# Loads of the float64 weight pieces begun by the POOL engine on a queue of its own instead of the sync engine's queue

## The chip, the cores and the metric

One core of a Trainium2 chip runs the kernel: TensorE (PE) multiplies, VectorE (DVE) and ScalarE (ACT) do elementwise work, GpSimd (POOL) does small extra work, and SyncE (SP) does nothing but start transfers. All of them work on one on-chip memory; 16 DMA engines move data between it and the chip's main memory. The metric is the device time of one execution in microseconds, lower is better.

## The reference, cut to what matters

```python
def _attn_ref(q, k, v, n_sink, window):          # 4 x 8 heads, 768 positions, 64 wide
    scores = scale * np.matmul(q, k.transpose(0, 1, 3, 2))
    keep = is_sink | in_window                   # 4 sinks, window of 128
    scores = np.where(keep, scores, -1000000000.0)
    ... # softmax
    return np.matmul(a, v).astype(np.float32)

x = attention output as 3072 tokens x 512
h = np.maximum(x @ w_in, 0.0)                    # 512 -> 2048
x = (h * h @ w_out).astype(np.float32)           # 2048 -> 512
a = x @ w1; b = x @ w2                           # 512 -> 1024 each
h = a * b @ w3                                   # 1024 -> 1024
out = (h @ w_out2).astype(np.float32)            # 1024 -> 512
```

q, k and v arrive as float32. All weights arrive as float64.

## The kernel before, in words

The kernel runs attention, the first feed-forward network and the second one for all 3072 tokens, in blocks of up to 512 tokens. The work overlaps: attention of later tokens runs on PE, DVE and ACT while the first network already works on block 0 (from about 100 to 200 us), and while blocks 1 and later follow (to about 687 us). Between about 687 and 760 us weights of the second network are folded together, and from there to the end the second network runs.

[...] `f32_piece` (L1015 to L1030) takes a buffer named `raw64` and starts the transfer of one piece of 512 x 128 float64 numbers (512 KB, read as pairs of int32) into it. `conv` then makes float32 numbers of it with `f64_to_f32_up` (L80 to L99): ACT takes the upper word (L86), DVE makes exponent and sign from the 16-bit parts (L91 and L94), and DVE joins them (L97). `split` then makes two float16 parts of the result, a high and a low one, and these are what PE multiplies with. Every second `w_in` piece has its low part made by POOL (L801).

There are two `raw64` buffers, so the transfer of a piece can start only when the piece two before it has been read by ACT (L86) and DVE (L94). 64 pieces go this way: 16 of `w_in`, 16 of the first `w_out`, 8 of the second `w_out`, and 24 of `w1`, `w2` and `w3` together. The even pieces of `w3` have a loader of their own (`load_w3`, L1176, buffer `raw_w`), which the change doesn't touch.

All transfers of the kernel are started by SP, in one order: the loads of q, k and v (L506, L518), the transposing transfers of keys (L555), of queries (L594) and of the softmax weights (L738), the weight pieces (L1029), a spill and a reload, and the output. An instruction of SP that waits holds up all that stand behind it. The same is true of POOL, which clears parts of `vp` (L599), copies the sink columns of the keys (L612, L615, L947) and makes the low parts (L801).

Line 288 is a helper: PE, ACT and DVE instructions that go through it are listed under that line, whatever they do, so they are told apart by the names of their tiles. Of these, `hps` is the first network's hidden product, `sc` the attention scores, `pr` and `stt` the softmax with its statistics, `ph` its result in float16, `pt` the transpose of `ph`, `y` the attention output and `xn` its normalized form (made by DVE, which frees the bank in which the next `y` is summed up). The helper also keeps PE, ACT and DVE in the order of the program from block 0 of the first network on. The conversions call the engines directly, and their place among the rest is chosen by a scheduler that plays the program through with a model of each engine's times; so is the order on SP and POOL.

Of the kernel before, what the change touches and what calls it, by code (L numbers as in the profile page):

```python
# [296 lines left out]
def kernel(  # L297
# [16 lines left out]
    POOL, SP = nc.gpsimd, nc.sync  # L314
# [51 lines left out]
    with ExitStack() as fast:  # L366
# [6 lines left out]
        def slab(tag, shape, dt, name, bufs=1):  # L373
            return big.tile(shape, dt, tag=tag, name=name, bufs=bufs)
# [642 lines left out]
        def f32_piece(src, dst=None, name="cv"):  # L1017

            if src.dtype == F32:
                if dst is None:  # L1020
                    dst = slab("t2", [128, 512], F32, name, bufs=T2B)
                SP.dma_start(out=dst, in_=src)
                return dst
            raw = slab("raw64", [128, 512, 2], I32, "raw64", bufs=2)
            fl = raw.rearrange("p n c -> p (n c)")
            sb32 = src.bitcast(I32)
            if len(sb32.shape) == 3:
                fl = fl.rearrange("p (a c) -> p a c", a=sb32.shape[1])
            SP.dma_start(out=fl, in_=sb32)  # L1029
            return raw  # L1030

        def conv(raw, dst=None):
# [15 lines left out]
        def load_wi(j):  # L1048
            raw_w["wi", j] = f32_piece(
                w_in[:, j * 128:(j + 1) * 128].rearrange("(c p) f -> p c f", p=128)  # L1050
            )
# [9 lines left out]
        def load_wo(j):  # L1061
            raw_w["wo", j] = f32_piece(w_out[j * 128:(j + 1) * 128, :])
# [87 lines left out]
        def load_wo2(j):  # L1150
            raw_w["wo2", j] = f32_piece(w_out2[j * 128:(j + 1) * 128, :])
# [269 lines left out]
        for h in range(2):  # L1421
            SP.dma_start(
                out=vsf[h * NSINK:(h + 1) * NSINK, :, h, :],
                in_=v[0].rearrange("(a h2) s d -> h2 s a d", h2=2)[h, 0:NSINK],
# [193 lines left out]
```

## Time and profile before

| | us |
|---|---|
| median of 3 runs (lowest to highest) | 1110.32 (1108.42 to 1110.94) |
| the profiled execution | 1110.19 |
| its span in the trace | 1108.0 |
| PE busy | 1045.3 (94%) |
| DVE busy | 750.3 (68%) |
| ACT busy | 709.4 (64%) |
| POOL busy | 45.0 (4%), 163 instructions |

The profile is of one execution. Its span runs from the first to the last instruction, and 2.2 us of the execution lie outside it. Busy time of an engine is the time in which it worked on instructions; the start of a transfer isn't counted in it. Where the trace shows idle time ahead of an instruction, it names what ended last before it could begin: "[2.26 <-DMA raw]" reads "idle for 2.26 us, until the transfer into `raw` had landed". The trace drops the numbers at the end of buffer names and the 64 of `raw64`, so `raw<-in_moe_w_out_dram` is a weight piece.

### The profile page before, as it was taken

How to read it: one execution, taken by the hardware profiler on the slowest of the kernel's cores; microseconds unless marked ns; L12 is line 12 of the kernel's file. 1: busy time of each engine (PE TensorE's matmuls, PEld its weight loads, DVE VectorE, ACT ScalarE, POOL GpSimd, SP SyncE). 2: the span in 40 equal slices, each digit the busy share in tenths (PEclk: the TensorE clock that was granted, in tenths of full speed). 3: DMA queues.
4: the chain of work that ended last, by engine and by line, in shares of the span. 5: the costliest groups of instructions: out<-in, count | busy, mean ns of one | idle time of the engine just before them, and what ended most of it. 6: DMA issues, size and time to landing. Idle time of an engine off the chain costs nothing. (4 is left out here: it accounts for less than half of the span.)

```text
span 1108.0 us, 20449 instructions
## 1 busy us (share of the span) xinstructions
PE 1045.3 (94%) x7146; PEld 636.4 (57%) x7146; DVE 750.3 (68%) x2292; ACT 709.4 (64%) x1836; POOL 45.0 (4%) x163
## 2 busy tenths in 40 slices
PE   6777897999999999999999998999999999999996
PEld 5665443555555555555554444457767776777774
DVE  8797888887788888877865667945363636453433
ACT  6975688887667666766754877854464546454532
POOL 2110111000000000000000000000000000000000
PEclk9867999999999999999999999999999999999998
DMA  8876787786567657556833324421020201010101
GB/s 189 157 157 140 179 204 184 150 183 122 104 144 145 117 107 173 118 114 144 147 68 99 115 96 140 164 75 40 2 77 1 77 1 39 1 39 1 38 1 41
DMA packets 265535, 113.46 MB, mean 102 GB/s; under 512 B 237648, under 2 KB 254032, under 8 KB 264784
## 3 DMA queue, kind: packets, MB, share of 16 engines
q1 hardware_dynamic: 265136, 111.55, 43.7%
q8 instruction: 58, 0.95, 0.4%
q14 instruction: 53, 0.43, 0.2%
q10 hardware_dynamic: 288, 0.52, 0.1%
HBM read 62.08 MB, written 11.53 MB: 66 GB/s over the span
## 5 line engine op out<-in xcount | busy, mean ns | idle before, releaser
L288 PE MATMUL hps<-xT,wi 128*128 128x512 f16 x1152 | 270.9, 386 | 0.0
L288 PE MATMUL x1ps<-g,wo 128*128 128x512 f16 x1152 | 265.6, 380 | 3.0 <-ACT g L288 2.0
L288 PE MATMUL cps<-x1T,w 128*128 128x256 f16 x2016 | 231.5, 273 | 7.2 <-DVE cq L288 4.6
L288 PEld LDWEIGHTS <-w 128*128 128x128 f16 x2016 | 196.9, 98 | 44.5 <-issue 9.1
L288 PEld LDWEIGHTS <-wi 128*128 128x128 f16 x1152 | 115.0, 100 | 123.2 <-issue 8.6
L288 PEld LDWEIGHTS <-wo 128*128 128x128 f16 x1152 | 109.8, 98 | 122.6 <-issue 5.7
L288 PE MATMUL ops<-w,h 128*128 128x512 f16 x576 | 133.5, 379 | 1.8 <-ACT h L288 1.8
L288 ACT ACTIVATE cp<-cps 128x256 f32<-128x256 f32 x96 | 36.1, 376 | 131.3 <-PE cps L288 131.3
L288 ACT ACTIVATE r<-hps 128x512 f32<-128x512 f32 x96 | 56.8, 592 | 94.7 <-PE hps L288 94.7
L288 ACT ACTIVATE pr<-pr,stt 128x264 f32<-128x264 f32 (+1 forms) x176 | 77.6, 483 | 32.9 <-DVE stt L288 31.5
L288 PEld LDWEIGHTS <-h 128*128 128x128 f16 x576 | 56.2, 98 | 58.1 <-ACT h L288 2.1
L288 DVE TENSOR_TENSOR ph<-pr,ph 128x512 f16<-128x512 f32 (+2 forms) x148 | 59.2, 436 | 35.2 <-ACT ph L288 33.2
L288 DVE SCALAR_TENSOR_TENSOR asb<-cq,cps 128x256 f32<-128x256 f32 x48 | 20.2, 420 | 87.6 <-PE cps L288 87.6
L288 DVE CUSTOM_DVE_ANT_0 pr<-sc,mask 128x264 f32<-128x264 f32 (+1 forms) x176 | 65.2, 400 | 16.1 <-PE sc L288 15.5
L288 PEld LDWEIGHTS <-pt 128*128 128x128 f16 x956 | 40.3, 98 | 34.5 <-issue 17.1
L288 ACT ACTIVATE ph<-pr 128x512 f16<-128x512 f32 (+2 forms) x148 | 55.9, 421 | 5.8 <-DMA pt<-ph 3.4
L288 ACT ACTIVATE g<-r 128x512 f16<-128x512 f32 x88 | 55.3, 629 | 2.4
L288 DVE TENSOR_TENSOR g<-r,g 128x512 f16<-128x512 f32 x56 | 38.6, 689 | 24.6 <-ACT g L288 24.4
L97 DVE SCALAR_TENSOR_TENSOR cvy<-cvy,cvt 128x512 int32<-128x512 int32 x72 | 49.1, 688 | 8.5 <-ACT cvy L86 8.3
L288 PE MATMUL y<-vp,pt 128*128 128x65 f16 (+1 forms) x888 | 40.6, 195 | 14.7 <-DVE xn L288 14.6
L288 DVE TENSOR_TENSOR h<-asb,h 128x512 f16<-128x512 f32 x48 | 33.2, 691 | 28.2 <-ACT h L288 28.2
L288 PEld LDWEIGHTS <-qT 128*128 128x128 f16 x592 | 41.4, 99 | 18.9 <-issue 0.7
(193 smaller groups left out, 1490.3 us busy)
## 6 DMA issues: line engine op xcount, KB each, us to landing
raw<-in_moe_w_out_dram SPq DMA_DIRECT2D x24, 512.0 KB
raw<-in_moe_w_dram SPq DMA_DIRECT2D x24, 512.0 KB
raw<-in_moe_w_in_dram SPq DMA_DIRECT2D x16, 512.0 KB
raw<-in_k_dram SPq DMA_DIRECT2D x84, 64.0 KB
raw<-in_q_dram SPq DMA_DIRECT2D x84, 64.0 KB
raw<-in_v_dram SPq DMA_DIRECT2D x84, 64.0 KB
x_dr<-x1e SPq DMA_DIRECT2D x20, 256.0 KB
x1s<-x_dr SPq DMA_DIRECT2D x5, 1024.0 KB
```

Of the source, the lines that this page charges most:

```text
L97: nc.vector.scalar_tensor_tensor(out=dst, in0=y, scalar=3, in1=t, op0=ALU.logical_shift_left, op1=ALU.bitwise_or)
L288: r = f(*args, **kw)
```

## The change

One line of `f32_piece` changes. The loads of the 64 pieces are started by POOL and no longer by SP. What is read, the buffers, the conversions and all other transfers stay as they are.

```diff
             sb32 = src.bitcast(I32)
             if len(sb32.shape) == 3:
                 fl = fl.rearrange("p (a c) -> p a c", a=sb32.shape[1])
-            SP.dma_start(out=fl, in_=sb32)
+            POOL.dma_start(out=fl, in_=sb32)
             return raw
```

On POOL, the instructions of the first half of block 0 (about 112 to 136 us) are these before: `vp` is cleared, and `ks` and `kT` are the sink columns of the keys.

```order
L615 COPY kT_1601<-ks_705 128x4x8
L599 MEMSET vp_1810 128x2x2
L599 MEMSET vp_2429 128x2x2
L615 COPY kT_2011<-ks_914 128x4x8
L612 COPY ks_1908<-kT_1804 128x32
L615 COPY kT_1806<-ks_1908 128x4x8
```

After the change the same stretch of POOL reads as follows.

```order
L615 COPY kT_1601<-ks_705 128x4x8
L1029 DMA raw64_1620<-in_moe_w_out_dram 128x1024
L599 MEMSET vp_1810 128x2x2
L1029 DMA raw64_1721<-in_moe_w_out_dram 128x1024
L1029 DMA raw64_1731<-in_moe_w_in_dram 128x4x256
L599 MEMSET vp_2429 128x2x2
L1029 DMA raw64_1824<-in_moe_w_out_dram 128x1024
L615 COPY kT_2011<-ks_914 128x4x8
L612 COPY ks_1908<-kT_1804 128x32
L615 COPY kT_1806<-ks_1908 128x4x8
L1029 DMA raw64_1927<-in_moe_w_out_dram 128x1024
L1029 DMA raw64_1937<-in_moe_w_in_dram 128x4x256
```

Six loads have come in between the six small instructions, in the order of the pieces; the small instructions keep their order.

On SP, the stretch of block 0 from about 146 to 160 us reads as follows before. `kT`, `qT` and `pt` are transposing transfers, `raw_2102` are pieces of q, k and v, and `raw64` the weight pieces.

```order
L555 DMA_TRANSPOSE kT_2011<-pkk_1911 128x4x128
L555 DMA_TRANSPOSE kT_2013<-pkk_1911 128x4x128
L594 DMA_TRANSPOSE qT_2015<-pkq_1912 128x4x128
L738 DMA_TRANSPOSE pt_1960<-ph0_101 128x4x128
L1029 DMA raw64_2032<-in_moe_w_out_dram 128x1024
L1029 DMA raw64_2133<-in_moe_w_out_dram 128x1024
L506 DMA raw_2102<-in_k_dram 128x2x64 x2
L506 DMA raw_2102<-in_q_dram 128x2x64 x2
L506 DMA raw_2102<-in_v_dram 128x2x64 x2
L1029 DMA raw64_2143<-in_moe_w_in_dram 128x4x256
L738 DMA_TRANSPOSE pt_2061<-ph1_102 128x9x128
```

After the change the same stretch, with its first instructions and some more at its end:

```order
L555 DMA_TRANSPOSE kT_2013<-pkk_1911 128x4x128
L594 DMA_TRANSPOSE qT_2015<-pkq_1912 128x4x128
L738 DMA_TRANSPOSE pt_1960<-ph0_101 128x4x128
L506 DMA raw_2102<-in_k_dram 128x2x64 x2
L506 DMA raw_2102<-in_q_dram 128x2x64 x2
L506 DMA raw_2102<-in_v_dram 128x2x64 x2
L738 DMA_TRANSPOSE pt_2061<-ph1_102 128x9x128
L555 DMA_TRANSPOSE kT_2216<-pkk_2118 128x4x128
L555 DMA_TRANSPOSE kT_2218<-pkk_2118 128x4x128
L594 DMA_TRANSPOSE qT_2220<-pkq_2119 128x4x128
```

The weight pieces are gone from SP, and the other transfers stand as they did. `raw64_2032` no longer stands behind the transposes.

On DVE, the start of the program (about 10.5 to 13.5 us) has the masks and the first softmax, and the first piece's conversion behind them, before:

```order
L288 TENSOR_SCALAR mask_143<-m0_135 128x128
L288 TENSOR_SCALAR mask_147<-m2_133 128x264
L288 SCALAR_TENSOR_TENSOR vp_532<-raw_171,vp_532 128x2x64
L288 TENSOR_SCALAR mask_145<-m1_134 128x264
L288 ISA pr_229,stt_230<-sc_225,mask_143 128x128
L288 ISA stt_230 128x1
L288 ISA pr_229,stt_230<-sc_227,mask_143 128x128
L288 ISA stt_230 128x1
L288 TENSOR_SCALAR stt_230<-stt_230 128x2
L91 TENSOR_SCALAR cvt_238<-raw64_183 128x512
L94 TENSOR_SCALAR cvt_238<-raw64_183 128x512
```

After the change the conversion of the first piece stands a few rows further up, and that of the second piece stands among the masks:

```order
L288 TENSOR_TENSOR m0_135<-m2_133,snk_130 128x128
L288 TENSOR_SCALAR vs_1089<-sel_78 128x4
L91 TENSOR_SCALAR cvt_249<-raw64_185 128x512
L94 TENSOR_SCALAR cvt_249<-raw64_185 128x512
L288 COPY m2_133<-snk_130 128x8
L288 TENSOR_TENSOR m1_134<-m2_133,snk_130 128x128
L288 MEMSET m1_134 128x8
L288 TENSOR_SCALAR mask_143<-m0_135 128x128
L97 SCALAR_TENSOR_TENSOR cvy_248<-cvy_248,cvt_249 128x512
L288 TENSOR_SCALAR mask_147<-m2_133 128x264
L288 TENSOR_SCALAR mask_145<-m1_134 128x264
L288 ISA pr_229,stt_230<-sc_225,mask_143 128x128
```

Two conversions (`raw64_183` and `raw64_185`) have moved ahead of the first softmax, the row `pr_229`.

## Rows read from the trace of the kernel before

**Rows 1.** Busy time by stretch: us, PE, PEld, DVE, ACT, POOL, PEclk, DMA share, GB/s.
```profile
100.00:200.00 100.00, 85.67 (x572) 43.62 (x570) 86.88 (x279) 79.32 (x234) 10.29 (x24) 0.95 0.80 183
200.00:560.00 360.00, 360.00 (x2625) 192.33 (x2624) 291.06 (x1004) 256.84 (x656) 19.39 (x88) 1.00 0.67 135
560.00:687.00 127.00, 124.20 (x653) 58.01 (x649) 79.07 (x198) 87.90 (x193) 0.00 (x0) 1.00 0.33 95
687.00:760.00 73.00, 68.03 (x384) 38.94 (x385) 56.13 (x107) 47.17 (x100) 0.00 (x0) 0.98 0.37 130
```
**Rows 2.** Waits, 100 to 200 us: who waited for whom, us in total, times, longest.
```profile
PE y L288 <- DVE xn L288: 13.4, 5, 3.6
DVE cvt L91 <- DMA raw<-in_moe_w_out_dram: 9.8, 5, 2.9
```
**Rows 3.** Timeline of DVE, conversions: start, us, instruction, idle before it.
```profile
115.34 0.46 DVE L94 TENSOR_SCALAR cvt<-raw 128x512 uint16<-128x512 uint16 x1
123.19 0.47 DVE L91 TENSOR_SCALAR cvt<-raw 128x512 uint16<-128x512 uint16 x1 [2.26 <-DMA raw<-in_moe_w_out_dram]
...
146.50 0.44 DVE L94 TENSOR_SCALAR cvt<-raw 128x512 uint16<-128x512 uint16 x1
156.22 0.47 DVE L91 TENSOR_SCALAR cvt<-raw 128x512 uint16<-128x512 uint16 x1 [2.48 <-DMA raw<-in_moe_w_out_dram]
...
175.63 0.45 DVE L94 TENSOR_SCALAR cvt<-raw 128x512 uint16<-128x512 uint16 x1
184.59 0.47 DVE L91 TENSOR_SCALAR cvt<-raw 128x512 uint16<-128x512 uint16 x1 [2.94 <-DMA raw<-in_moe_w_out_dram]
```
**Rows 4.** Timeline of SP's queue, starts of transfers in block 0.
```profile
115.14 2.50 SPq L555 DMA_TRANSPOSE kT<-pkk  x2
117.74 1.21 SPq L594 DMA_TRANSPOSE qT<-pkq  x1
119.05 0.52 SPq L1029 DMA_DIRECT2D raw<-in_moe_w_out_dram  x1
...
152.21 1.05 SPq L1029 DMA_DIRECT2D raw<-in_moe_w_out_dram  x2
...
180.44 0.52 SPq L1029 DMA_DIRECT2D raw<-in_moe_w_out_dram  x1
```
**Rows 5.** Timeline of PE, the first two of the five waits for xn.
```profile
109.52 0.81 PE L288 MATMUL y<-vp,pt 128*128 128x65 f16 x12 [3.60 <-DVE xn L288]
...
132.17 0.34 PE L288 MATMUL y<-vp,pt 128*128 128x65 f16 x6 [2.79 <-DVE xn L288]
```
**Rows 6.** Timeline of POOL in block 0.
```profile
110.63 2.41 POOL L801 TENSOR_TENSOR wi<-cvy,wi 128x512 f16<-128x512 f32 x1 [10.46 <-ACT wi L288]
...
117.45 0.12 POOL L599 MEMSET vp<- 128x4 f16 x1 [4.26 <-PE y L288]
```
**Rows 7.** Groups by line and form: count, busy, mean ns of one, idle before.
```profile
L801 POOL TENSOR_TENSOR wi<-cvy,wi 128x512 f16<-128x512 f32 x8 | 10.7, 1337 | 46.1 <-ACT wi L288 46.1
...
L97 DVE SCALAR_TENSOR_TENSOR cvy<-cvy,cvt 128x512 int32<-128x512 int32 x72 | 49.1, 688 | 8.5 <-ACT cvy L86 8.3
```
**Rows 8.** Timeline of the start, SP's queue and DVE.
```profile
8.65 0.94 SPq L1029 DMA_DIRECT2D raw<-in_moe_w_in_dram  x2
...
12.30 0.28 DVE L288 CUSTOM_DVE_ANT_0 pr<-sc,mask 128x128 f32<-128x128 f32 x1
```
**Rows 9.** Waits of DVE, 0 to 100 us, the largest line.
```profile
DVE cvt L91 <- DMA raw<-in_moe_w_in_dram: 4.7, 3, 2.1
```
**Rows 10.** Timeline of DVE in block 0, two multiplications of one shape.
```profile
111.32 1.76 DVE L288 TENSOR_TENSOR ph<-pr,ph 128x512 f16<-128x512 f32 x2
...
158.10 0.78 DVE L288 TENSOR_TENSOR ph<-pr,ph 128x512 f16<-128x512 f32 x2
```
**Rows 11.** Timeline of the fold, SP's queue and ACT.
```profile
687.15 3.64 SPq L1029 DMA_DIRECT2D raw<-in_moe_w_dram  x2
...
695.69 0.68 ACT L86 ACTIVATE cvy<-raw 128x512 f32<-128x512 f32 x1
```

## The prediction

> **What bounds the kernel now.** I read the table of stretches first. From 200 to 560 us PE is busy for all 360.00 us, so nothing that happens to a weight piece there can shorten the time [rows 1]. The stretch that is open is 100 to 200 us, block 0 of the first network beside the rest of attention: PE is busy for 85.67 of 100 us, DVE for 86.88, ACT for 79.32, POOL for 10.29. No engine is full, so it is bound by waits between engines, with DVE nearest to full. The list of waits then says whom PE waits for there: for `xn` of DVE, 13.4 us in five waits [rows 2], nearly all of the 14.33 us in which PE is not busy. In the same list DVE waits 9.8 us, five times, for a weight piece to land. DVE works in order, so an `xn` behind a waiting conversion is late.
>
> Why are these pieces late? The timelines of DVE and SP side by side tell. The second-last conversion ahead of a wait frees the buffer, at the end of its L94: 115.34 + 0.46 = 115.80, 146.50 + 0.44 = 146.94, 175.63 + 0.45 = 176.08 [rows 3]. SP begins the loads that need these buffers at 119.05, 152.21 and 180.44 [rows 4], so 3.25, 5.27 and 4.36 us later. Until then it stands in order behind other transfers: ahead of 119.05 behind two transposes of keys (2.50 us) and one of queries (1.21 us). From its begin to DVE's use a load takes 123.19 - 119.05 = 4.14, 4.01 and 4.15 us [rows 3, 4].
>
> **The change part by part.** *Removed from SP.* SP no longer begins the weight pieces. Its remaining transfers stand in the old order, each up to about 0.5 us earlier per load removed [rows 4]; I count nothing for it, since PE waits for no transpose in the list of waits' large lines.
>
> *Added to POOL.* A load is now begun by POOL, which is free for 90 of 100 us of block 0 [rows 1]. In its order each load stands behind small instructions only, so POOL is mostly there when the buffer comes free. What a begin by POOL costs more than one by SP, call it e, no row shows. The lower end is 0 (it starts as SP's, 0.52 us [rows 4]); the upper end is POOL's longest instruction in block 0, 2.41 us [rows 6]; I take the mean of its wide instruction, 1.34 us [rows 7], since preparing a transfer over 128 partitions is nearest to a piece of work over 128 partitions.
>
> Gain of each wait: the smaller of the wait and (the delay less e).
> - 123.19: wait 2.26, delay 3.25 less 1.34 = 1.91. Gain 1.91.
> - 156.22: wait 2.48, delay 5.27 less 1.34 = 3.93. Gain 2.48.
> - 184.59: wait 2.94, delay 4.36 less 1.34 = 3.02. Gain 2.94.
> - The other two waits are 9.82 - 7.68 = 2.14 us together (five waits, of which three have rows) [rows 2, 3]. I take half, 1.07.
>
> That is 8.40 us on DVE. Not all of it is seen by PE: its first waits for `xn` are at 109.52 and 132.17 [rows 5], and none lies in the 8.98 us behind 123.19, so PE had work then, and the 1.91 us are not counted. What is left is 6.5 us (6.49). With e = 0 the same sum is 2.48 + 2.94 + 2.14 = 7.6; with e = 2.41 it is 2.48 + 1.95 = 4.4, the small ones gone. What is late next is DVE itself, 86.88 us of work in what would be some 93 us.
>
> *The start.* Two conversions move ahead of the first softmax on DVE: four passes of about 0.46 us and two of 0.69 us [rows 3, 7], 3.2 us. The first softmax, at 12.30 before [rows 8], is later by up to that. The work is then missing further on; as no row of the first 100 us stands here but DVE's waits, I take DVE's share of idle time from the stretch next to it (13 of 100 [rows 1]) and a little more for the gaps of a start: a fifth of 3.2 us is not given back, +0.6. The ends: +3.2 if none is given back, and -4.7 if the three waits for `w_in` pieces in the first 100 us all go [rows 9] because the pieces start earlier than SP's 8.65 [rows 8].
>
> *POOL and DVE at once.* The same form of DVE multiplication takes 1.76 us for two at 111.32 and 0.78 us at 158.10 [rows 10]; at 111.32 POOL's L801 is running, from 110.63 for 2.41 us instead of its mean 1.34 [rows 6, 7]. So a wide POOL instruction and a DVE multiplication lengthen each other, by 1.0 us. Does a load's begin do that too? 18 pieces are begun in block 0. At the lower end none meets, 0; at the upper end all do, 18.0 us. I take a third of them, 6, at the 0.12 us of POOL's small memset [rows 6], as what a begin writes is nearer to that than to a 128x512 tile: +0.7.
>
> A rule of the Trainium skill speaks against the change here. "SBUF — State Buffer", section "SBUF: two separate sides", says in its box on the DVE-blocks-DMA trap that a transfer begun by GpSimd has its descriptors written by GpSimd, which cannot write them while DVE runs certain two-port operations, and advises a begin from ACT or SP. The pair of rows on `ph` agrees that the two engines hold each other up, and no run here shows it for a begin. By that rule the upper end of this term is the right one.
>
> *POOL's own work behind waiting loads.* POOL now waits in its queue for buffers. Behind such a wait stand memsets of `vp` and copies of sink columns. The memset at 117.45 waited 4.26 us for PE itself [rows 6], so it keeps its time as long as the load ahead of it begins at 115.80. Zero; a few tenths if not.
>
> *Later stretches.* 200 to 560 us: zero, PE is full [rows 1]. 560 to 687 us: PE is busy 124.20 of 127 us, which leaves 3 us to lose or gain. Fold: the second of the two loads at 687.15 to 690.79 is used at 695.69 [rows 11], at least 4.9 us after its begin and so 0.8 us more than the 4.1 a load takes; 1.34 is 0.5 us over that. PE idles 5 of 73 us there [rows 1], and the pieces are not what it waits for, so +0.2, with ends 0 and +1.
>
> *Sum.* Against the profiled execution, 1110.19 us (span 1108.0, and 2.2 outside), which is 0.1 us below the median of the runs: 1110.2 - 6.5 + 0.6 + 0.7 + 0.2 = **1105.2 us**. Its own range by these ends is 1098 (-7.6 and -4.7) to 1109 (-4.4 and +3.2).
>
> **The rivals.** *The transfer lands later, by as much as it begins earlier.* If a load of POOL takes 4.1 us longer to land, twice what SP's takes, the gains are 5.27 - 4.1 = 1.2 and 4.36 - 4.1 = 0.3, and pieces that just arrive now begin to be waited for, at about the same price: 1110 us, within 1108 and 1112. For it: the two queues share 16 DMA engines that are busy 80% of block 0 [rows 1], and no row shows a load by POOL. Against it: the engines are no busier than before, and what SP lost was time in line.
>
> The Trainium skill, "DMA: Bandwidth & Descriptors", section "Issuing engines are not separate DMA queues", says that starting transfers on several engines saves only the sequencer's time to start them, usually small beside the transfer. Taken as SP's own begin of 0.52 us per bound load it would give 2.6 us at most, so about 1108, which is this rival. The trace speaks half against it: it is SP's place in line, 3.25 to 5.27 us, that is long.
>
> *DVE and POOL hold each other up (the slower side).* If every begin costs a DVE instruction what L801 cost at 111.32, 1.0 us, DVE has 86.9 + 18.0 = 104.9 us of work in block 0's 100, so the stretch grows by 5 us and the gain is gone; the loads of the first 100 us add some 2 us. 1117 us. It decides from (100 - 86.9) / 18 = 0.7 us per load on. For it: the pair of rows; DVE is busy nearly always, so each begin meets something. Against it: L801 reads and writes whole tiles, a begin doesn't.
>
> *The load isn't begun earlier.* POOL could be held in its order by its own waits (for PE, for a transposed `kT`) as SP is by its transposes, or the two conversions moved ahead cost 3.2 us for good: 1109 to 1114. The order speaks against the first, as the loads stand behind copies that ran long before.
>
> **How the numbers follow.** Forecast 0.45, later landing 0.22, held up 0.25, not begun earlier or something else 0.08. A measurement of this kernel tells about 0.2% from no change, 2.2 us: faster is below 1108.1, slower above 1112.5. Faster is 0.45 plus a third of the second case, 0.07: 0.52. Slower is 0.25, 0.02 of the second and half of the last: 0.31. Same is the rest, 0.17. The range goes from 1097 (the start's waits all gone, too) to 1118 (held up, with 1 us more), and the forecast's own is 1098 to 1109.
>
> **What the new profile would show.** Right: in 100 to 200 us DVE's wait for `raw` falls from 9.8 to below 3 us, PE's wait for `xn` from 13.4 to about 7, and PE's busy share of the stretch rises. The time from a buffer's release to its load's begin falls from 3 to 5 us to below 1.5. Wrong, by the second case: begins early, but DVE's wait for `raw` is as long as now. Wrong, by the third: DVE's wait for `raw` is small, but its instructions of one form are longer than before (two `ph` nearer 1.76 than 0.78), and its busy time in block 0 is well above 87. The fourth: the begin stands late on POOL's timeline, or the first softmax is 3 us late and nothing is won back. What overturns most would be a change in 200 to 560 us: PE idle there.

## The result, and the profile after

The changed kernel takes 1095.41 us (median of four runs, 1094.44 to 1095.95) against 1110.63 us of the kernel before; the ratio is 0.9858, with a 95% interval of 0.9829 to 0.9887. It is 15 us faster where 5 were forecast, and the time lies below the lower end of the range, 1097. The profiled execution of the changed kernel takes 1095.90 us and spans 1094.0, so the span is 14.0 us shorter.

First, where the time went. The busy time by stretch of the changed kernel, in the columns of [rows 1]:

```profile
0.00:100.00 100.00, 73.51 (x468) 59.84 (x469) 86.24 (x378) 75.26 (x267) 27.91 (x67) 0.88 0.76 165
100.00:200.00 100.00, 93.69 (x652) 48.53 (x650) 93.09 (x308) 87.89 (x257) 23.33 (x46) 0.98 0.95 201
200.00:560.00 360.00, 360.00 (x2625) 192.52 (x2623) 290.47 (x1001) 253.74 (x643) 24.27 (x92) 1.00 0.65 132
560.00:687.00 127.00, 122.54 (x608) 57.35 (x607) 84.01 (x189) 92.07 (x199) 13.40 (x20) 0.99 0.37 118
```

From 100 to 200 us PE is now busy for 93.69 us and DVE for 93.09, against 85.67 and 86.88 [rows 1]. POOL's busy time rises from 10.29 to 23.33 us; a begin by POOL is counted as busy time, one by SP is not. From 200 to 560 us PE has been full both times.

Stretches of equal length hold different work in the two kernels, so I cut them by work: from PE's first `hps` to its 241st score product, an event near 200 us in both. First the kernel before, then the changed one (same columns):

```profile
0.00:94.60 94.60, 69.40 (x420) 59.26 (x421) 77.25 (x358) 70.64 (x253) 14.90 (x50) 0.81 0.79 166
94.60:202.10 107.50, 93.17 (x605) 46.93 (x604) 91.10 (x291) 83.02 (x243) 10.68 (x27) 0.93 0.78 179
```
```profile
0.00:91.80 91.80, 65.31 (x419) 55.69 (x420) 80.16 (x358) 70.39 (x253) 26.51 (x64) 0.88 0.79 173
91.80:187.20 95.40, 89.26 (x607) 45.99 (x605) 89.54 (x292) 83.06 (x243) 24.05 (x47) 0.97 0.89 199
```

The start is 2.8 us shorter and block 0 is 12.1 us shorter. All the gain is there: every PE event from 210 us on comes 14.6 us sooner than before, to within 0.1 us, up to the fold, and the second network keeps that.

In block 0 the count of DVE's instructions agrees (291 and 292), and its time adds up as busy and idle: busy 91.10 before and 89.54 after, idle 16.4 and 5.9. Its work is the same: instruction by instruction, overlaps not taken off, it sums to 112.9 and 112.8 us. The waits of DVE in that stretch of the changed kernel (who waited for whom, us in total, times, longest):

```profile
DVE pr L288 <- PE sc L288: 1.2, 1, 1.2
DVE ph L288 <- ACT ph L288: 1.0, 2, 0.7
DVE wo L288 <- ACT wo L288: 0.7, 1, 0.7
DVE xT L288 <- ACT xT L288: 0.7, 1, 0.7
DVE cvt L91 <- DMA raw<-in_moe_w_out_dram: 0.7, 2, 0.3
```
```profile
PE y L288 <- DVE xn L288: 6.0, 6, 2.2
```

The wait for weight pieces, 9.8 us [rows 2], is 0.7: 9.1 of the 12.1 us. PE's wait for `xn`, in the second fence, falls from 13.4 [rows 2] to 6.0.

PE's own time falls too, from 93.17 to 89.26 us for the same products, and its granted clock rises from 0.93 to 0.97; busy time times clock is 86.6 in both. So these 3.9 us are the clock, which is a mix of its two levels, 1.2 and 2.4 GHz. These are its stretches at 1.2 GHz by waits of PE for `xn`, three before and one after (the columns of [rows 1]):

```profile
109.10:112.50 3.40, 2.98 (x19) 1.63 (x19) 3.40 (x9) 3.08 (x9) 1.87 (x1) 0.50 0.93 245
133.00:136.40 3.40, 3.40 (x10) 1.20 (x9) 3.40 (x12) 2.44 (x7) 0.60 (x2) 0.50 0.50 122
170.50:173.90 3.40, 3.40 (x10) 1.22 (x8) 2.74 (x8) 3.13 (x9) 1.92 (x3) 0.50 0.99 242
```
```profile
104.80:108.20 3.40, 3.40 (x19) 1.52 (x16) 3.40 (x7) 2.59 (x8) 2.23 (x2) 0.50 0.93 293
```

The three before begin within 1 us of the end of a wait for `xn` (3.60 us until 109.52, 2.79 until 132.17 [rows 5], 2.81 until 169.65), the one after behind a wait of 2.15 us until 104.56. Before, PE also comes into block 0 at the low level, until 98.8 us; after, it does so until 94.5.

The conversions that answer to [rows 3], and POOL's begins that answer to SP's in [rows 4]:

```profile
110.58 0.45 DVE L94 TENSOR_SCALAR cvt<-raw 128x512 uint16<-128x512 uint16 x1
116.25 0.46 DVE L91 TENSOR_SCALAR cvt<-raw 128x512 uint16<-128x512 uint16 x1
138.12 0.45 DVE L94 TENSOR_SCALAR cvt<-raw 128x512 uint16<-128x512 uint16 x1
143.91 0.56 DVE L91 TENSOR_SCALAR cvt<-raw 128x512 uint16<-128x512 uint16 x1 [0.34 <-DMA raw<-in_moe_w_out_dram]
```
```profile
111.58 0.55 POOL L1029 DMA_DIRECT2D raw<-in_moe_w_out_dram  x1 [3.50 <-ACT r L288]
139.11 0.55 POOL L1029 DMA_DIRECT2D raw<-in_moe_w_out_dram  x1 [5.98 <-DVE g L288]
```

The buffers come free at 110.58 + 0.45 = 111.03 and 138.57, and POOL begins 0.55 and 0.54 us later, where SP took 3.25 and 5.27. Over all 18 pieces of block 0 the delay from release to begin has a mean of 0.52 us and a longest of 0.93; before, it was 1.62 and 5.27. From its begin to DVE's use the second load takes 143.91 - 139.11 = 4.80 us, and the other load that DVE still waits for 5.63 (begun at 157.40, used at 163.03). By SP it was 4.0 to 4.15 for the three in [rows 4].

### The profile page after: what moved, and what is told of

Read it like the earlier page. It is cut to its first block, busy times and chain, and to the rows that moved or that the text cites. A ratio compares the mean times of both kernels' runs of the same rounds, so it can differ in the third digit from the quotient of the medians.

```text
span 1094.0 us, 20464 instructions
## 1 busy us (share of the span) xinstructions
PE 1038.5 (95%) x7146; PEld 633.2 (58%) x7146; DVE 752.4 (69%) x2292; ACT 709.0 (65%) x1836; POOL 90.0 (8%) x227
## 2 busy tenths in 40 slices
DMA packets 253248, 113.46 MB, mean 104 GB/s; under 512 B 237648, under 2 KB 237648, under 8 KB 252496
## 3 DMA queue, kind: packets, MB, share of 16 engines
q0 software_dynamic: 9216, 33.56, 9.7%
## 5 line engine op out<-in xcount | busy, mean ns | idle before, releaser
L288 PE MATMUL x1ps<-g,wo 128*128 128x512 f16 x1152 | 265.2, 380 | 2.0 <-ACT g L288 2.0
L288 PE MATMUL hps<-xT,wi 128*128 128x512 f16 x1152 | 267.1, 382 | 0.0
L288 PE MATMUL cps<-x1T,w 128*128 128x256 f16 x2016 | 232.9, 274 | 7.1 <-DVE cq L288 4.6
L288 PEld LDWEIGHTS <-w 128*128 128x128 f16 x2016 | 198.0, 98 | 44.7 <-issue 8.8
L288 PEld LDWEIGHTS <-wi 128*128 128x128 f16 x1152 | 114.2, 99 | 120.2 <-issue 3.7
L288 PEld LDWEIGHTS <-wo 128*128 128x128 f16 x1152 | 109.9, 98 | 121.3 <-issue 4.2
L288 PE MATMUL ops<-w,h 128*128 128x512 f16 x576 | 133.5, 379 | 1.8 <-ACT h L288 1.8
L288 ACT ACTIVATE cp<-cps 128x256 f32<-128x256 f32 x96 | 36.1, 376 | 132.6 <-PE cps L288 132.6
L288 ACT ACTIVATE r<-hps 128x512 f32<-128x512 f32 x96 | 56.8, 592 | 93.1 <-PE hps L288 93.0
L288 ACT ACTIVATE pr<-pr,stt 128x264 f32<-128x264 f32 (+1 forms) x176 | 77.5, 483 | 28.7 <-DVE stt L288 28.6
L288 PEld LDWEIGHTS <-h 128*128 128x128 f16 x576 | 56.3, 98 | 58.1 <-ACT h L288 2.1
L288 DVE TENSOR_TENSOR ph<-pr,ph 128x512 f16<-128x512 f32 (+2 forms) x148 | 58.9, 436 | 35.6 <-ACT ph L288 32.3
L288 DVE SCALAR_TENSOR_TENSOR asb<-cq,cps 128x256 f32<-128x256 f32 x48 | 20.2, 420 | 88.1 <-PE cps L288 88.1
L288 DVE CUSTOM_DVE_ANT_0 pr<-sc,mask 128x264 f32<-128x264 f32 (+1 forms) x176 | 65.2, 400 | 15.5 <-PE sc L288 15.1
L288 ACT ACTIVATE ph<-pr 128x512 f16<-128x512 f32 (+2 forms) x148 | 55.9, 421 | 4.6 <-DMA pt<-ph 2.2
L288 ACT ACTIVATE g<-r 128x512 f16<-128x512 f32 x88 | 55.4, 629 | 2.5
L288 PEld LDWEIGHTS <-pt 128*128 128x128 f16 x956 | 39.9, 98 | 28.6 <-issue 10.9
L288 DVE TENSOR_TENSOR g<-r,g 128x512 f16<-128x512 f32 x56 | 38.5, 688 | 23.7 <-ACT g L288 23.7
L97 DVE SCALAR_TENSOR_TENSOR cvy<-cvy,cvt 128x512 int32<-128x512 int32 x72 | 48.9, 686 | 8.5 <-ACT cvy L86 8.4
L288 DVE TENSOR_TENSOR h<-asb,h 128x512 f16<-128x512 f32 x48 | 33.2, 691 | 28.3 <-ACT h L288 28.3
L288 DVE TENSOR_TENSOR cr<-cq,cps 128x256 f32<-128x256 f32 x48 | 20.2, 420 | 47.0 <-ACT cq L288 47.0
L288 PEld LDWEIGHTS <-qT 128*128 128x128 f16 x592 | 40.7, 98 | 18.7 <-issue 0.7
```

The costliest lines, as they stand in the source:

```text
L97: nc.vector.scalar_tensor_tensor(out=dst, in0=y, scalar=3, in1=t, op0=ALU.logical_shift_left, op1=ALU.bitwise_or)
L288: r = f(*args, **kw)
```

## The experiments

Theory 1: what pays is that a piece's load begins as soon as its buffer is free, in the 100 us in which DVE sets the pace. Rivals: SP's other transfers gain because SP is relieved; POOL's queue moves the pieces in larger packets; the pieces of the start are what counts; or any queue apart from SP's will do. The column "block 0" is the length of the stretch by work, "delay" the mean from release to begin over the 18 pieces, "waits" DVE's waits for pieces, "PE" its busy time in block 0 with its granted clock, all from one profiled execution. "n" counts the runs; each ratio is to runs of the kernel before in the same rounds.

| kernel | us, median (n) | ratio, 95% interval | first hps | block 0 | delay | waits | PE |
|---|---|---|---|---|---|---|---|
| before | 1110.6 | | 94.6 | 107.5 | 1.62 | 9.8 | 93.2 (0.93) |
| changed | 1095.4 (4) | 0.9858, 0.9829 to 0.9887 | 91.8 | 95.4 | 0.52 | 0.7 | 89.3 (0.97) |
| changed, later | 1097.4 (5) | 0.9873, 0.9847 to 0.9899 | 93.2 | 96.9 | 0.53 | 0.9 | 90.8 (0.95) |
| pool_late | 1100.9 (4) | 0.9930, 0.9902 to 0.9957 | 95.0 | 98.1 | 0.53 | 1.3 | 91.6 (0.94) |
| pool_early | 1107.0 (10) | 0.9972, 0.9958 to 0.9985 | 92.0 | 104.9 | 1.59 | 9.7 | 90.2 (0.96) |
| sp_bufs3 | 1097.1 (4) | 0.9887, 0.9865 to 0.9909 | 96.7 | 95.7 | 3.87 | 2.1 | 86.9 (0.99) |
| pool_rows | 1100.6 (4) | 0.9928, 0.9910 to 0.9946 | 93.3 | 96.7 | 0.70 | 2.4 | 88.8 (0.97) |
| act_queue | 1106.4 (10) | 0.9953, 0.9936 to 0.9970 | 97.3 | 101.1 | 1.31 | 3.4 | 89.9 (0.96) |
| hold2 | 1105.6 (7) | 0.9950, 0.9933 to 0.9966 | 94.0 | 102.1 | 2.97 | 5.1 | 87.9 (0.99) |
| hold4 | 1126.2 (4) | 1.0150, 1.0123 to 1.0177 | 94.2 | 122.1 | 6.32 | 9.8 | 96.5 (0.91) |
| pool_from2 | 1100.2 (5) | 0.9923, 0.9893 to 0.9954 | 95.2 | 95.9 | 0.49 | 1.7 | 89.1 (0.97) |
| pool_halves | 1098.6 (4) | 0.9895, 0.9867 to 0.9922 | 93.3 | 95.2 | 0.60 | 1.6 | 87.0 (0.99) |
| pool_bufs3 | 1093.2 (4) | 0.9853, 0.9827 to 0.9878 | 91.2 | 93.1 | 0.51 | 0 | 87.9 (0.98) |
| pool_bufs3, later | 1095.7 (5) | 0.9865, 0.9841 to 0.9888 | 91.7 | 95.1 | 0.52 | 0 | 89.3 (0.97) |

The changed kernel's two profiles differ by 1.4 us in the first `hps` and by 1.5 in block 0; less than that can't be told from one profile. Against the kernel before, block 0 shrinks by at least what DVE's waits shrink by in every kernel but hold4. What it shrinks by beyond the waits (0.9 to 4.6 us, hold2, hold4 and act_queue left aside) goes with PE's shorter busy time (1.6 to 6.3 us less), so with its clock. No run sets the clock alone.

A rival that isn't in the list is the scheduler's new order. Of the 20 conversions of block 0, 10 stand at another place among DVE's instructions of L288 than before, by 1 to 6 places. act_queue has 16 of the 20 where the changed kernel has them, and its block 0 is 101.1 us long with 3.4 us of waits, so these places alone don't give the gain. How much they add isn't separated.

**pool_late and pool_early: which stretch pays.** `n_p` counts the pieces.

```diff
-            POOL.dma_start(out=fl, in_=sb32)
+            (POOL if n_p >= 14 else SP).dma_start(out=fl, in_=sb32)
```

pool_early has `n_p < 14`. Expected of pool_late:

> The first 14 pieces begun by SP as before, the other 50 by POOL. Theory 1 (the loads of block 0 begin 3 to 5 us sooner, DVE's waits for pieces go, and DVE sets the pace there): the changed kernel won 12.1 us between the first hps and the 241st score product, and 2.8 us ahead of it. This kernel keeps the 12.1 and not the 2.8: 1098 us. Rival (the start matters, as it sets when the later pieces stand in line): less than half of the gain, over 1103 us.

Expected of pool_early:

> The first 14 pieces begun by POOL, the other 50 by SP as before. Theory 1: only the 2.8 us of the first 95 us, so 1107 to 1108 us, and DVE's waits for pieces in block 0 still near 9.8 us. Rival (the start matters): over half of the gain, below 1103 us.

pool_late's block 0 is 98.1 us long, so it keeps 9.4 of the 12.1 us, and nothing of the start (95.0): 1100.9, between the 1098 expected and the rival's 1103, and by the ratios about half of the gain. pool_early keeps the start (92.0) and DVE's wait line in block 0 stays as it was:

```profile
DVE cvt L91 <- DMA raw<-in_moe_w_out_dram: 9.7, 5, 3.3
```

Its 1107.0 us is what theory 1 said. But its block 0 is 2.6 us shorter than before although the waits there are not, and PE's busy time in it is 3.0 us less, at a clock of 0.96 instead of 0.93. So block 0's 12.1 us divide: some 9.4 come with the late pieces, most of it DVE's waits, and some 2.6 with the early ones. Most of the gain is block 0's. The two kernels' gains, 0.0070 and 0.0028 by the ratios, fall short of the whole, 0.0142 and later 0.0127, by 3 to 5 us, which neither shows alone.

**sp_bufs3: an earlier begin without POOL.** In the kernel before:

```diff
-            raw = slab("raw64", [128, 512, 2], I32, "raw64", bufs=2)
+            raw = slab("raw64", [128, 512, 2], I32, "raw64", bufs=3)
```

> The kernel before with three raw64 buffers instead of two, all loads by SP. A piece can begin one conversion earlier. Theory 1 (it is the late begin alone): DVE's waits for pieces in block 0 fall from 9.8 to below 2 us, and the time to 1096 to 1101 us without POOL. Rival (POOL's own queue, its larger packets or SP's relief are what pays): 1107 us or more.

Its waits of DVE in block 0 (96.7 to 192.4 us), the first line, and the stretch by work:

```profile
DVE cvt L91 <- DMA raw<-in_moe_w_out_dram: 2.1, 3, 1.4
```
```profile
96.70:192.40 95.70, 86.92 (x605) 44.96 (x604) 88.95 (x295) 83.16 (x243) 11.51 (x27) 0.99 0.96 196
```

SP still begins late, 3.87 us behind the release on average, but with a third buffer the release comes one conversion sooner. The waits shrink to 2.1 us, block 0 is as short as in the changed kernel, and the time, 1097.1, can't be told from the changed kernel's, as the intervals of the ratios overlap. No queue of POOL's and no packet of its is needed for the gain of block 0. This is the clearest test of the cause.

**pool_rows: only the pieces that were waited for.** `w_out` and odd `w3` pieces by POOL, pieces of 1 KB runs by SP:

```diff
-            POOL.dma_start(out=fl, in_=sb32)
+            (POOL if len(sb32.shape) == 2 else SP).dma_start(out=fl, in_=sb32)
```

> Only the pieces with rows of 4 KB (w_out of both networks, odd w3) are begun by POOL, those of 1 KB runs (w_in, w1, w2) by SP as before. All five waits of block 0 are for w_out pieces. Theory 1: nearly the whole 12 us of block 0, 1097 to 1101 us. Rival (POOL's queue moves 1 KB runs in packets of 4 KB, and this pays): below 3 us of gain, 1107 us or more.

1100.6 us and 96.7 in block 0. These pieces have rows of 4 KB with either engine, so larger packets are not the cause of block 0's gain. The time stands 3 to 5 us above the changed kernel's, and what the other pieces' begin and what their packets add to that isn't separated.

**hold2 and hold4: the load late again, SP still relieved.**

```diff
+            if 14 <= n_p < 32:
+                for _ in range(4):
+                    POOL.memset(raw.rearrange("p n c -> p (n c)"), 0)
             POOL.dma_start(out=fl, in_=sb32)
```

hold2 has two memsets. Expected of hold2:

> The changed kernel, with two POOL memsets of the whole raw64 buffer ahead of each of the 18 loads from the 15th to the 32nd piece. They need the free buffer and the load needs them, so each load begins some 2 us later; SP is as relieved as in the changed kernel. Theory 1 (the begin alone counts): the begin stands 2.6 instead of 0.5 us behind the buffer's release, near the 2.6 to 3.3 us of the smaller delays before; a third of block 0's gain goes, 1098 to 1102 us, and DVE's waits for pieces are some 3 us. Rival (it is SP's other transfers that gain from SP's relief): no loss, 1094 to 1097 us.

Expected of hold4:

> The same with four memsets, some 4 us later. Theory 1: the begin stands 4.7 us behind the release, as late as the three late ones of the kernel before (3.3, 5.3 and 4.4), for every piece and not for five of 18; the whole gain of block 0 goes, 1106 to 1116 us, with DVE's waits for pieces near 10 us or more. Rival (SP's relief): 1094 to 1099 us.

hold2 loses about two thirds of the gain, hold4 all of it and 16 us more: 1105.6 and 1126.2 us, both beyond what theory 1 said, and the delays (2.97 and 6.32 us) are longer than planned, since POOL's other work gets in between. Two costs are mixed here. DVE's waits for pieces come back, 5.1 and 9.8 us. And DVE itself gets slower beside POOL's memsets. The groups of DVE in block 0 of hold4 (count, busy, mean ns, idle before):

```profile
L91 DVE TENSOR_SCALAR cvt<-raw 128x512 uint16<-128x512 uint16 x20 | 13.3, 666 | 10.0 <-DMA raw<-in_moe_w_out_dram 5.8 <-DMA raw<-in_moe_w_in_dram 4.0
L94 DVE TENSOR_SCALAR cvt<-raw 128x512 uint16<-128x512 uint16 x19 | 11.4, 601 | 0.0
```

L91 takes 666 ns here and 456 before. SP is as relieved here as in the changed kernel, so the rival's "no loss" is out; how much of hold4's loss is delay and how much is the memsets isn't separated. Block 0 is 26.7 us longer than in the changed kernel: DVE's busy time is 11.9 of them (101.4 against 89.5), its waits for pieces 9.1.

**act_queue: another queue than SP's and POOL's.**

```diff
-            POOL.dma_start(out=fl, in_=sb32)
+            ACT.dma_start(out=fl, in_=sb32)
```

> All 64 loads begun by ACT instead of SP or POOL. It is another queue than SP's too, but ACT is busy for 79 of 100 us of block 0 and works in order. Theory 1 (what pays is that the begin comes right after the buffer's release): ACT comes to a load late, and each costs ACT some 0.5 us: between the kernel before and the changed one, 1100 to 1112 us. Rival (any queue apart from SP's will do): 1094 to 1098 us.

1106.4 us: a third of the gain. ACT comes to a load 1.31 us behind the release on average, and 3.4 us of waits are left. That SP is rid of the pieces isn't enough: on an engine that is busy, the begin is late again. A begin takes ACT's queue some 0.33 to 0.47 us as well, and what that costs ACT's own work isn't separated. (Its first `hps` is also the latest, 97.3.)

**pool_from2: the start.** As pool_late, but `n_p >= 2`.

> The first two pieces by SP as before, the other 62 by POOL. In the changed kernel PE waits 4.77 us for a piece of k at the start (1.31 before), since two weight pieces of 512 KB are begun ahead of it, and its first y comes 5.7 us later; by 95 us it is 2.7 us ahead. If the start's loss is for good, this kernel keeps 3 to 5 us of it: 1090 to 1092 us. If early first pieces are what wins the time back by 95 us: 1095 to 1098 us, no faster than the changed kernel.

1100.2 us: slower than the changed kernel, the second expectation and a little beyond. PE waits 1.89 us for that piece of k instead of 4.77, and its 31st score product comes at 23.8 us (25.8 in the changed kernel, 23.1 before), yet the first `hps` comes at 95.2 instead of 91.8 or 93.2, and DVE waits for a `w_in` piece again, once for 4.0 us. The early pair costs time in the first 25 us and pays it back by 92 us.

**pool_halves: does a begin by POOL cost DVE anything?** Two transfers of half a piece each, so 128 begins.

> The changed kernel with each piece loaded by two transfers of 256 KB, so 128 begins by POOL instead of 64. If a begin by POOL lengthens DVE's work beside it, as the mean of DVE's ph over 128x512 says (689 ns before, 771 changed, 683 with three buffers and SP), that mean goes to 850 ns, and the time up by 2 to 6 us, 1097 to 1101 us. If begins cost DVE nothing outside of the start: 1094 to 1097 us, since each transfer is half as long.

1098.6 us, 1.2 over the changed kernel in the same rounds, with intervals that overlap; the time lies within the first expectation, so the time alone decides nothing. L97, the instruction that stands beside begins most often, over the whole program: first the kernel before is [rows 7], 688 ns; then the changed kernel, then pool_halves:

```profile
L97 DVE SCALAR_TENSOR_TENSOR cvy<-cvy,cvt 128x512 int32<-128x512 int32 x72 | 48.9, 686 | 8.5 <-ACT cvy L86 8.4
```
```profile
L97 DVE SCALAR_TENSOR_TENSOR cvy<-cvy,cvt 128x512 int32<-128x512 int32 x72 | 49.7, 696 | 8.8 <-ACT cvy L86 8.7
```

686 and 696 ns, when in the changed kernel 53 of the 72 overlap with a begin (these 53 take 685 on average, the other 19 take 687), and when sp_bufs3, where POOL begins nothing, has 696 as well. My expectation took the changed kernel's longer `ph` (771 against 689 ns) for the price of a begin. It isn't: the timeline of the changed kernel's `ph` has one long pair and 0.77 us for the others, and the long pair stands beside an L801 again:

```profile
106.37 1.74 DVE L288 TENSOR_TENSOR ph<-pr,ph 128x512 f16<-128x512 f32 x2
121.05 0.77 DVE L288 TENSOR_TENSOR ph<-pr,ph 128x512 f16<-128x512 f32 x2
```
```profile
105.85 1.61 POOL L801 TENSOR_TENSOR wi<-cvy,wi 128x512 f16<-128x512 f32 x1 [1.53 <-ACT wi L288]
```

Not every instruction of DVE goes free. The small `stt` in block 0 are longer in the changed kernel, two of them, beside begins, by far (399 and 385 ns); first the kernel before, then the changed one:

```profile
L288 DVE TENSOR_SCALAR stt<-stt 128x2 f32<-128x2 f32 x14 | 2.3, 162 | 0.0
```
```profile
L288 DVE TENSOR_SCALAR stt<-stt 128x2 f32<-128x2 f32 x14 | 2.8, 202 | 0.0
```

And at the start of pool_halves a cast on DVE takes 2.18 us (0.73 before) with nothing but begins on POOL beside it:

```profile
3.53 2.18 DVE L288 CAST rel<-col_i 128x264 f32<-128x264 int32 x1
```
```profile
3.19 3.03 POOL L1031 DMA_DIRECT2D raw<-in_moe_w_in_dram  x4
```

**pool_bufs3: both together.** The changed kernel with `bufs=3`, run twice, the second time beside the changed kernel.

> The changed kernel with three raw64 buffers. Theory 1: DVE's waits for pieces are at 0.7 us already, so a third buffer has nothing left to take away: 1093 to 1096 us. If the two add up (a rival by which SP's three buffers and POOL's begin win different time): 1085 us or less.

> The changed kernel with three raw64 buffers once more, beside the changed kernel itself in the same five rounds. If the 2.2 us between their medians (1093.2 and 1095.4) is real, it is 1092 to 1094 us here and 1 to 3 us below the changed kernel; if the third buffer has nothing to take away, the two are within 1 us.

Expected of the changed kernel beside it:

> The changed kernel itself, as the partner of the kernel with three buffers: 1094.4 to 1096 us, as in its first runs.

First 1093.2, then 1095.7 (ratio 0.9865, 0.9841 to 0.9888) beside 1097.4 of the changed kernel. It is 1.7 us below its partner, and the intervals cover each other, so whether the difference is real stays open. The changed kernel's own 1097.4 lies above the 1094.4 to 1096 expected of it. The two gains do not add up (that would have been 1085 or less), and a version that beats the changed kernel beyond doubt was not found.

## Why the prediction was wrong

**Right:** the stretch, the direction and the mechanism. 9.1 of the 9.8 us of DVE's waits are gone, POOL begins right behind the release, nothing is won or lost from 200 us on, and the rival in which begins and DVE hold each other up in block 0 for 1.0 us each didn't come true. That e came out near was luck: 1.34 was taken from a wide instruction of POOL, while what showed is a begin 0.5 us behind the release and a load that took 0.7 to 1.5 us longer from begin to use (4.80 and 5.63 against 4.1), 1.2 to 2.0 together.

**The step that failed first: the sum of the waits' gains, 6.5 us, where block 0 gained 12.1** (10.6 by the changed kernel's second profile). Two cuts were wrong.
- "The 1.91 us are not counted", since PE had work behind that wait. But DVE works in order, and what it loses in one place makes all its later work late: PE's cover at that moment only delays when PE sees it. The very next wait, 2.79 us at 132.17 [rows 5], shows it: the same product waits 0.13 us in the changed kernel. That DVE, nearest to full and waited for in all of PE's long waits, sets the pace is borne out by the table, where block 0 gains no less than DVE's waits lose.
- Half of the two small waits was taken away without their rows. They are 1.38 us at 107.24 (delay 2.57) and 0.76 at 129.79 (delay 2.87), so with e at 1.34 the prediction's own rule gives 1.23 + 0.76 = 1.99. Both went.

That makes 9.1 us. The other 3 us (1.7 by the second profile) belong to a term that the prediction put at nothing: PE's own time. It took PE's work as fixed and only its waits as open, but PE's busy time in block 0 fell by 3.9 us with its clock (2.4 in the second profile). pool_early has 2.6 us of gain in block 0 with DVE's waits as before and PE's busy time 3.0 us less. That SP's transposes come sooner and the scheduler's new order may be in it as well; no run separates them.

**The step that failed second: the start, +0.6 where it was -2.8.** The upper end's loss did happen: PE's first `y` comes at 22.5 us instead of 16.8, more than the 3.2 us allowed, but not by the conversions moved ahead alone. Two other causes show. PE waits longer for a piece of k, begun beside 1 MB of weights (changed kernel):

```profile
11.91 1.20 PE L288 MATMUL kqps<-ident,raw 128*128 128x128 f32 x4 [4.77 <-DMA raw<-in_k_dram]
```

And a cast on DVE lasts 3.17 us instead of 1.15. Two begins push POOL's two wide memsets back from 3.17 to 4.85 us, and the cast then runs beside them (first the kernel before, then the changed one with POOL's work):

```profile
4.30 1.15 DVE L288 CAST snk<-ki_i 128x128 f32<-128x128 int32 x1
```
```profile
4.48 3.17 DVE L288 CAST snk<-ki_i 128x128 f32<-128x128 int32 x1
```
```profile
3.19 1.67 POOL L1029 DMA_DIRECT2D raw<-in_moe_w_in_dram  x2
4.85 2.07 POOL L1431 MEMSET ph<- 128x1152 f16 x2
```

But the lower end's mechanism happened as well, and it is the larger: DVE's waits for `w_in` pieces in the first 100 us, 4.7 us [rows 9], are gone, and from 40 to 60 us DVE is busy 18.57 of 20 us (14.49 before). pool_from2 speaks for it that the two hang together: without the early pair by POOL its 31st score product is late by 0.7 us and not by 2.7, and its first `hps` isn't early. I had both ends in hand and took a fraction of one.

**Contention, +0.7.** Near zero in block 0: the `stt` above cost 0.6 us more there, and DVE's instructions together no more than before (112.8 and 112.9 us). The pair of rows that carried the rival [rows 10] was misread. Its two instructions are not of one shape: the row joins one of 128x512 and one of 128x16, and at 111.32 it is the small one that is longer, 1.16 us instead of 0.18, ending at 113.08 when L801 ends at 113.04. The row shows DVE beside a wide POOL instruction, not beside a begin, and hold4 shows it again. The Trainium skill, "SBUF — State Buffer", section "SBUF: two separate sides", warns that GpSimd cannot write a transfer's descriptors while certain DVE operations run. In block 0 no trace here shows begins held up so: most took 0.53 to 0.76 us and the longest 1.15, with DVE busy 93 of 100 us. By that warning it is the load that would be late, so it bore on e rather than on this term; what does show here is the other side, DVE's `stt` and casts longer beside begins.

**The other rule.** The Trainium skill, "DMA: Bandwidth & Descriptors", section "Issuing engines are not separate DMA queues", says that another issuing engine saves only the time to start a transfer. Transfers did not get faster here (4.80 against 4.1 us), which agrees. But what was saved is not the time to start one: it is the time for which a load stood in line on SP ahead of its start, up to 5.27 us.

## What to carry to other kernels

Where a load's begin trails the release of its buffer by more than the engine's own start, look at what stands ahead of it in the queue; a free queue or one more buffer removed most of the same wait here, and only one of them was needed. When the waiting engine is the one nearest to full, count all of its removed waits, whatever its consumers were doing at the moment. Where PE's waits fall, look at its granted clock as well: its own time may not be fixed. And where a term of the start has two ends of opposite sign, weigh both mechanisms instead of a fraction of one.

## What the runs showed of the hardware

- POOL's queue moved pieces of 1 KB runs in packets of 4 KB: the packets between 512 B and 2 KB, 254032 - 237648 = 16384 before, are gone in the changed kernel, and its software queue has 9216 packets for 33.56 MB. It didn't show in the time.
- A begin by POOL took about 0.55 us for a piece with rows of 4 KB and 0.76 for one of 1 KB runs. DVE's L97 beside one was as fast as alone (685 and 687 ns), its `stt` of 128x2 took up to 399 ns instead of 162, and a cast of int32 at the start of pool_halves 2.18 us instead of 0.73. Memsets of 128x1024 int32 on POOL lengthened DVE's L91 from 456 to 666 ns on average.
- TensorE's granted clock ahead of the first `hps` was 0.88 in the changed kernel (0.89 later) and 0.91 with pool_early; with the first pair by SP it was 0.79 to 0.83 (before and pool_rows 0.81, pool_late and pool_from2 0.83, sp_bufs3 0.79). act_queue, with the first pair by ACT, had 0.86 and yet the latest `hps`. From 60 to 80 us it was 0.82 in the changed kernel and 0.63 before, so both spent a part of it at 1.2 and a part at 2.4 GHz; ahead of that, from 40 to 60 us, PE was busy 14.66 of 20 us in the changed kernel and 13.15 before. How much of the start's 2.8 us comes from this and how much from the earlier pieces stays open.
